# Second-phase weight sums formed during attention and kept in DRAM, x stored in 384-token pieces, eight output tiles in both passes

## The chip, the cores and the metric

The kernel runs on one core of a Trainium2 chip. The metric is the device time of one execution in microseconds. The engines are TensorE (PE in the profile, with its weight loads as PEld), VectorE (DVE), ScalarE (ACT), GpSimd (POOL, which here only issues accumulating DMAs) and SyncE (SP, which issues all other DMAs). Each engine, and each queue of DMA issues, works in the order in which its instructions were written.

## The reference

Linear attention with an exponential feature map (8 batches, 8 heads, 576 tokens, 64 dimensions, 128 features), and then a gated layer on the 4608 tokens of 512 features:

```python
def phi(x):
    proj = np.einsum('bhsd,df->bhsf', x, w_phi)
    proj = proj - np.max(np.abs(proj), axis=-1, keepdims=True)
    return np.concatenate([np.exp(proj), np.exp(-proj)], axis=-1)
q_p, k_p = (phi(q), phi(k))
kv = np.einsum('bhsf,bhsd->bhfd', k_p, v)
z = np.sum(k_p, axis=2)
num = np.einsum('bhsf,bhfd->bhsd', q_p, kv)
den = np.einsum('bhsf,bhf->bhs', q_p, z)[..., None] + 1e-06
...
gate = 1.0 / (1.0 + np.exp(-(x @ w_gate)))
val = x @ w_val
return (gate * val @ w_out).astype(np.float32)
```

The hidden width is 1536, twelve tiles of 128, called j = 0 to 11. The weights of the layer arrive as 64-bit floats.

## The kernel before

*Precision.* Every product of the gated layer is made of three matmuls: a value is split into a high part (a ScalarE copy that rounds) and a low part (a VectorE subtraction), and high x high, high x low and low x high are summed. `weigh` turns a raw 64-bit weight tile (512 KB, `raw`) into high and low with mask and shift operations on VectorE and two ScalarE operations.

*First phase.* There are 32 attention steps, one for a batch and a pair of heads (`attend`). The result x of a step goes to DRAM (`xscr`, the tile xs). As soon as 512 tokens are complete, `load_x` fetches them, splits them, sends high and low back to DRAM (`keep_x`, tile xparts), and `first_js` computes j = 0 to 3 for them, while attention goes on. Attention's last matmul stands at 516 us. Chunks 7 and 8 of the nine follow until about 617 us; I call this stretch the passage.

*Second phase.* The remaining eight j are taken in pairs n = 0 to 3, by a scheme with seven products in place of eight. For a pair and one of the three matrices m (gate, value, out), `combine` forms from two raw tiles, by sums and differences (lines L1103 to L1130), the high and low parts of seven weight blocks of 256 columns, one "sum" of 896 KB for each part. x enters in blocks of 768 tokens (two halves of 384): the four quarter blocks 11, 12, 21 and 22 give the seven operands 11, T1, T2, 21, T3, 22, T4 of the products (`x_blocks`). 11, 21 and 22 are fetched in high and low; the T operands are formed by VectorE (`less`, L1195; low part L1208) and ScalarE (L1204) from plain x. The 14 places for operands, `r_X`, hold one block and no more. The product matmuls all stand at L1250 (`group`); the copies that seed a product's bank are L1265 and the adds to a bank L1271.

Pass 1 runs n = 0, 1 over the six blocks (617 to 901 us), pass 2 runs n = 2, 3 (901 to 1200 us), starting with the block that pass 1 ended with, so that its x need not be fetched. A block is two gate groups, two value groups (the value group of the second pair is the last to read x) and four output groups (`sent`). An output group writes two tiles of 384 KB, which GpSimd adds to the output in DRAM with accumulating DMAs (L1404). In pass 1 the tiles (`r_w`) share places in the arena `flat` with gates and temporary values; in pass 2 eight tiles lie in an area of their own, `third`. Six sums are formed in the passage, for pass 1. One each is formed in the blocks 1 to 5 of pass 1 and stored to DRAM in both parts (`kept`, L1143), to be fetched for pass 2 (`fetched`, L1154); the twelfth is formed at the start of pass 2.

*Order.* Nothing is ordered by hand. `Plan.run` simulates the engines with costs per instruction and writes each engine's instructions in the order in which the simulation starts them; ranks decide between those that are ready. Buffers are places in arenas, which the simulation hands out as they come free.

The order of fetches before, in `x_blocks` (b11, b21 and b22, plain x, lie in the low halves of the operands of the same name):

```python
        b11, b21, b22 = (at_[n][1] for n in ("11", "21", "22"))
        fetch(b11, xscr, xmark, 0, 0)
        fetch(b12, xscr, xmark, 0, 1)
        fetch(b22, xscr, xmark, 1, 1)
        fetch(b21, xscr, xmark, 1, 0)
```

Of the kernel before, what the change touches and what calls it, by code (L numbers as in the profile page):

```python
# [39 lines left out]
RB = 61 << 10  # L40
FB = 10 << 10
SB = 14 << 10
# [18 lines left out]
KEEP = 10.0  # L61
SPAN = 46.0
PASS = 43.8
ACTN = 0.2

# [78 lines left out]
class Op:  # L144
    def __init__(self, eng, busy, lag, fn, rank, mode, slack, bufs, after):
        self.eng, self.busy, self.lag, self.fn = eng, busy, lag, fn
        self.rank, self.mode, self.slack, self.bufs = rank, mode, slack, bufs
        self.wait, self.then, self.ready, self.opens = len(after), [], 0.0, ()
        for a in after:
            a.then.append(self)  # L150


class Plan:
# [30 lines left out]
    def run(self):  # L184
        free = dict.fromkeys(self.NEAR, 0.0)
        ready = {e: [] for e in free}
        mode, wire, late = None, 0.0, 0
# [30 lines left out]
        while left:  # L218
            best = None
            for e, cs in ready.items():  # L220
# [3 lines left out]
                first = min(t for t, _ in ts) + (ACTN if late and e == 'ACT' else self.NEAR[e])  # L224
# [6 lines left out]
                t, o = min((x for x in ts if x[0] <= first), key=key)  # L231
# [10 lines left out]
            free[o.eng] = t + o.busy  # L242
            if o.eng in ("SP", "POOL"):
                wire = max(wire, t) + o.lag / self.RATE[late] * 1e-6
                end = wire + self.LAND[late]
            else:
                end = t + o.busy + o.lag
# [27 lines left out]
def attention_moe(  # L275
# [54 lines left out]
    for hd in range(2):  # L330
# [4 lines left out]
    xscr = dram.tile([P, NC4, NT], F32, tag="xs", name="xs")  # L335
    xparts = dram.tile([2, P, NC4, NT], F32, tag="xp", name="xparts")
    gscr = {
        (n, m): dram.tile([2, P, 7 * 2 * P], F32, tag=f"g{n}{m}", name=f"g{n}{m}")
        for n in range(2, 4)
        for m in range(3)  # L340
        if (n, m) != (3, 2)
# [7 lines left out]
    staged = arena("prep", "staged", SB, F32R)  # L349
# [10 lines left out]
    r_top = x.ring(2, DM, U32)  # L360
    x = low()
# [6 lines left out]
    r_stage = staged().ring(2, 7 * 2 * P)  # L368
    r_x7 = high(42).ring(2 * NC4, CW)
    r_O2 = r_O[:]  # L370
    r_O += r_stage
# [4 lines left out]
    r_f2 = r_f  # L376
    r_w = flat().ring(5, 2 * HT) + flat(15).ring(2, 2 * HT)
    r_w2 = third().ring(8, 2 * HT)
# [23 lines left out]
    def on_act(n, fn, reads, writes, rank, after=()):  # L402
        return plan.op("ACT", 0.08 + n / 1200, 0.17, fn, reads, writes, rank, after=after)
# [16 lines left out]

    def keep_x(c, p, bufs, r):

        for n, x in enumerate(bufs):
            sp(
                256 << 10,
                lambda n=n, x=x: nc.sync.dma_start(
                    xparts[n, :, p, c * CW : c * CW + CW], x().bitcast(F32)
                ),
                [x], [(pmark[c], (p, n))], r,
            )  # L430

    closing, opening, feeding, exps = [], [], [], []

    def attend(i):
        b, p = steps[i]
        r, slack = due(i), 0.1 if i < 2 * NP else 0.5
        early, on_pe = i < NP, i < NQ
        rk, rn = (r + 11, r + 18) if i < NP else (r + KOFF, r + NOFF)
        banks = [r_a, r_g] if early else [r_a]
# [354 lines left out]
        while t < S:  # L794
            c, o = divmod(b * S + t, CW)
            wd = min(CW - o, S - t)
            sp(
                wd * 512,
                lambda t=t, wd=wd: nc.sync.dma_start(
                    xscr[:, p, b * S + t : b * S + t + wd], xp()[:, t : t + wd]  # L800
                ),
                [xp], [(xmark[c], (p, b))], rn + 7,
            )
            t += wd

    def weigh(j, m, r, deep, wh, wl, ms, part, after=(), again=False):
# [23 lines left out]
        if deep:  # L830
# [24 lines left out]
        on_act(  # L855
            DM, lambda: act.copy(wh()[:, ms], top().bitcast(F32)), [top], [(wh, part)], r,
        )
# [9 lines left out]
        else:  # L867
# [23 lines left out]
            src, a, b_ = raw, 1, 0  # L891
        dve(
# [17 lines left out]
    def load_x(c, r, rings, after=()):  # L910
        for p in range(NP):
            xh, xl = Buf([x[0] for x in rings], [P, CW]), Buf([x[1] for x in rings], [P, CW])
            xs[c, p] = xh, xl
            sp(
                256 << 10,
                lambda p=p, xl=xl: nc.sync.dma_start(
                    xl().bitcast(F32), xscr[:, p, c * CW : c * CW + CW]
                ),
                [xmark[c % NCH]], [xl], r, after,
            )  # L920
# [114 lines left out]

    for i in range(N):
# [35 lines left out]
    last.opens = [a().cells for a in (high, more, staged)]  # L1072
# [9 lines left out]
    KH = 2 * P  # L1082
    combined = []

    def pair(n):
        return JA + 2 * n, JA + 2 * n + 1

    def combine(n, m, r, rings, after):

        gh, gl = Buf(rings, [P, 7 * KH]), Buf(rings, [P, 7 * KH])  # L1090
        w = Buf([r_sum], [P, 4 * KH])

        def of(b, i, n=1):
            return b()[:, i * KH : (i + n) * KH]

        for i, j in enumerate(pair(n)):
            weigh(
                j, m, r + 3 * i, False, gh, gl,
                slice(2 * i * KH, 2 * (i + 1) * KH), i, after + combined[-1:], True,
            )  # L1100
            o_ = dve(
                DM,
                lambda i=i: vec.tensor_tensor(  # L1103
                    of(w, 2 * i, 2), of(gh, 2 * i, 2).bitcast(F32),
                    of(gl, 2 * i, 2).bitcast(F32), op=ALU.add,
                ),
                [(gh, i), (gl, i)], [(w, i)], r + 5,
            )
            opened = opened if i else o_
        p12, p21 = (1, 2) if m < 2 else (2, 1)  # L1110
        for o, a, b, op in (
            (3, p21, 3, ALU.add),
            (p21, 0, p21, ALU.subtract),
            (0, 3, 0, ALU.subtract),
            (p12, p12, 0, ALU.subtract),
        ):
            dve(
                KH,
                lambda o=o, a=a, b=b, op=op: vec.tensor_tensor(
                    of(w, o), of(w, a), of(w, b), op=op  # L1120
                ),
                [], [w], r + 5.5,
            )
        for o, i, part in ((4, 3, 2), (p21, p21, p21 // 2), (5, 0, 3), (6, p12, 4)):
            on_act(
                KH, lambda o=o, i=i: act.copy(of(gh, o), of(w, i)), [w], [(gh, part)], r + 6
            )
            dve(
                KH,
                lambda o=o, i=i: vec.tensor_tensor(  # L1130
                    of(gl, o), of(w, i), of(gh, o).bitcast(F32), op=ALU.subtract
                ),
                [w, (gh, part)], [(gl, part)], r + 6,
            )
        combined.append(opened)
        return gh, gl

    def kept(bufs, where, mark, r):

        for n, x in enumerate(bufs):  # L1140
            sp(
                x.shape[1] << 9,
                lambda n=n, x=x: nc.sync.dma_start(where[n], x().bitcast(F32)),  # L1143
                [x], [(mark, n)], r,
            )

    def fetched(rings, width, where, mark, r, after=()):

        out = []
        for n in range(2):  # L1150
            x = Buf(rings, [P, width])
            sp(
                width << 9,
                lambda n=n, x=x: nc.sync.dma_start(x().bitcast(F32), where[n]),  # L1154
                [(mark, n)], [x], r, after,
            )
            out.append(x)
# [383 lines left out]
```

## Time and profile before

| | us |
|---|---|
| median of 3 runs (lowest, highest) | 1202.79 (1199.7, 1206.44) |
| the profiled execution, and its span | 1201.93, 1200.2 |
| first phase, to attention's last matmul | 0 to 516 |
| passage | 516 to 617 |
| pass 1 | 617 to 901 |
| pass 2 | 901 to 1200 |

Busy time is the union of an engine's instructions. A wait is idle time of an engine just before an instruction, put down to what released it last. A matmul shows some 0.34 us, but matmuls overlap, so the pace is read from counts and starts. The chain of waits follows the execution back from its last instruction.

### The profile page before, as it was taken

Reading aid. Unit: us, or ns where it says so; the run is one execution under the profiler, and the core shown is the slowest. Engines: PE = TensorE matmul, PEld = TensorE weight load, DVE = VectorE, ACT = ScalarE, POOL = GpSimd, SP = SyncE. Lnnn points to the kernel's source line nnn. Section 1 sums busy time; section 2 is a strip of 40 time slices with the busy share of each in tenths; the row PEclk is TensorE's granted clock in tenths of the full one; section 3 lists DMA queues with packets and bytes.
Section 4 is the critical chain, followed back from the end, with each engine's and each line's share of the span. In section 5 each row is a group of like instructions: output and inputs, shape, how many; then the busy total and the mean of one; then the engine's idle time right before and its main releaser. Section 6 shows DMA issues by size and latency. Waiting matters only on the chain.

```text
span 1200.2 us, 23363 instructions
## 1 busy us (share of the span) xinstructions
PE 1148.7 (96%) x8940; PEld 959.9 (80%) x8940; DVE 926.5 (77%) x1841; ACT 728.7 (61%) x1485; POOL 77.8 (6%) x94
## 2 busy tenths in 40 slices
PE   8989999999999999999999999799999898988988
PEld 6656667667776777778888989799899798988988
DVE  7998898888888787578899889497867575745746
ACT  6766776666666675435557667476655565645643
POOL 0000000000000000000001021110211202202010
PEclk9989999999999999999999999899999999998989
DMA  6863483645455362455647876868796827757371
GB/s 233 252 230 96 148 260 100 224 125 187 125 174 170 112 222 64 172 193 201 181 126 191 246 176 201 224 154 257 177 380 160 188 93 145 173 135 166 95 182 53
DMA packets 109784, 209.69 MB, mean 175 GB/s; under 512 B 19432, under 2 KB 54888, under 8 KB 109672
## 3 DMA queue, kind: packets, MB, share of 16 engines
q1 hardware_dynamic: 97000, 173.59, 43.5%
q0 software_dynamic: 12672, 34.61, 16.2%
q8 instruction: 70, 1.15, 0.4%
q14 instruction: 42, 0.34, 0.1%
HBM read 124.78 MB, written 83.24 MB: 173 GB/s over the span
## 4 chain that ended last, share of the span: by engine, by line
PE 63%; DVE 18%; DMA 14%; issue 3%; ACT 2%; POOL 0%; SPq 0%; DVEq 0%; POOLq 0%; ACTq 0%
PE gate L944 13%; PE bank L1250 13%; DMA low<-xparts 8%; PE gate L1250 7%; PE gate L1001 6%; PE bank L647 5%; PE bank L689 4%; PE bank L458 3%; DMA out<-flat 3%; DVE low L1352 3%; PE bank L707 2%; PE bank L944 2%; DVE flat L1195 2%; DVE flat L1271 2%; PE bank L563 2%
## 5 line engine op out<-in xcount | busy, mean ns | idle before, releaser
L1250 PE MATMUL bank<-low,high 128*128 128x384 f32 x1302 | 253.6, 345 | 25.2 <-DMA low<-xparts 21.0
L1250 PEld LDWEIGHTS bank<-low,high 128*128 128x128 f32 x1302 | 232.4, 193 | 33.4 <-DMA low<-xparts 24.0
L944 PE MATMUL gate<-low 128*128 128x512 f32 x708 | 173.8, 399 | 5.5 <-ACT low L784 4.5
L944 PEld LDWEIGHTS gate<-low 128*128 128x128 f32 x708 | 131.9, 191 | 38.0 <-issue 5.3
L1250 PE MATMUL gate<-low,high 128*128 128x384 f32 x714 | 143.6, 343 | 7.3 <-DMA low<-xparts 5.8
L1250 PEld LDWEIGHTS gate<-low,high 128*128 128x128 f32 x714 | 127.7, 192 | 11.0 <-DMA low<-xparts 7.7
L505 ACT ACTIVATE ek<-ek 128x512 f32<-128x512 f32 (+1 forms) x192 | 95.3, 527 | 19.9 <-DVE ek L493 18.9
L1404 POOL DMA_DIRECT2D out<-flat x48 | 42.1, 985 | 868.3 <-DMA low<-xparts 648.1
L1250 PE MATMUL bank<-low 128*128 128x384 f32 x397 | 88.8, 338 | 1.9 <-DVE flat L1271 1.7
L1001 PE MATMUL gate<-low 128*128 128x512 f32 x372 | 89.3, 394 | 0.0
L1001 PEld LDWEIGHTS gate<-low 128*128 128x128 f32 x372 | 68.6, 188 | 14.5 <-issue 1.0
L1349 ACT CAST low<-flat 128x384 fp32r<-128x384 f32 x127 | 61.0, 514 | 21.6 <-DVE flat L1358 19.2
L1250 PEld LDWEIGHTS bank<-low 128*128 128x128 f32 x397 | 70.2, 188 | 4.2 <-DVE flat L1271 2.9
L647 PE MATMUL bank<-ek,vin 128*32 128x256 f32 x1240 | 73.2, 381 | 0.2 <-DVE mb L729 0.2
L1271 DVE TENSOR_TENSOR flat<-bank,flat 128x384 f32<-128x384 f32 x95 | 51.5, 552 | 24.6 <-PE bank L1250 19.5
L647 PEld LDWEIGHTS bank<-ek,vin 128*32 128x32 f32 x1240 | 37.5, 110 | 38.7 <-issue 7.8
L1358 DVE TENSOR_TENSOR flat<-flat,bank 128x384 f32<-128x384 f32 x26 | 14.3, 552 | 64.5 <-PE bank L1250 64.1
L464 DVE TENSOR_REDUCE mk<-bank 128x4 f32<-128x512 f32 (+1 forms) x92 | 48.8, 555 | 19.5 <-PE bank L458 19.2
L1352 DVE TENSOR_TENSOR low<-flat,low 128x384 fp32r<-128x384 f32 x112 | 59.1, 551 | 2.9 <-ACT low L1349 2.7
L968 ACT CAST low<-flat 128x512 fp32r<-128x512 f32 x36 | 22.3, 619 | 53.5 <-DVE flat L993 45.4
L1265 ACT COPY bank<-bank 128x384 f32<-128x384 f32 x80 | 37.3, 466 | 24.8 <-PE bank L1250 22.4
L1343 DVE TENSOR_TENSOR flat<-flat 128x384 f32<-128x384 f32 x96 | 51.0, 552 | 0.3
(220 smaller groups left out, 2219.8 us busy)
## 6 DMA issues: line engine op xcount, KB each, us to landing
low<-xparts SPq DMA_DIRECT2D x66, 384.0 KB
out<-flat POOLq DMA_DIRECT2D x48, 384.0 KB, 9.0
xparts<-low SPq DMA_DIRECT2D x64, 256.0 KB
out<-third POOLq DMA_DIRECT2D x40, 384.0 KB, 9.4
low<-xs SPq DMA_DIRECT2D x33, 384.0 KB
more<-w_moe SPq DMA_DIRECT2D x24, 512.0 KB
kin<-k SPq DMA_DIRECT2D x32, 320.0 KB
qin<-q SPq DMA_DIRECT2D x32, 320.0 KB
```

What stands on the lines that cost most here:

```text
L464: vec.tensor_reduce(mx, pk, axis=AX.X, op=ALU.max, apply_absolute_value=True)
L505: lambda g=g, sg=sg: act.activation(ek[g]()[:, :, sg * F : sg * F + F], ek[g]()[:, :, F:], AF.Exp, scale=1.0 - 2.0 * sg,),
L647: nc.tensor.matmul(o_[o : o + Q, : 2 * F], vx()[:, 2 * t + hd, o % D : o % D + Q], (e0, e1)[hd][:, t, :] if t < 4 else e2[:, 0, :], start= ...
L689: nc.tensor.matmul(nm()[o : o + Q, :], w()[:, sg, o : o + Q], es[sg]()[:, o // D, cs], start=sg == 0, stop=sg == 1, tile_position=(0, o),)
L944: nc.tensor.matmul(o(), a()[:, ws], x(), start=cc + n == 0, stop=cc == NC4 - 1 and n == 2,)
L1001: nc.tensor.matmul(acc(), w()[:, ms], a(), start=first and i == 0, stop=last and i == 2)
L1250: nc.tensor.matmul(o()[:, :HT], s()[:, ws], y, start=first and n + cc + i_ == 0, stop=n == len(terms) - 1 and cc == steps - 1 and i_ == 2, ...
L1271: HT, lambda: vec.tensor_tensor(at_(), p()[:, :HT], q(), op=ALU.add),
L1343: HT, lambda: vec.tensor_tensor(o(), a(), b(), op=ALU.subtract),
L1349: on_act(HT, lambda: act.copy(hh(), y()), [y], [hh], -100.0, after)
L1352: lambda: vec.tensor_tensor(hl(), y(), hh().bitcast(F32), op=ALU.subtract),
L1404: lambda f=f, y=y: nc.gpsimd.dma_start(final(f, dc), flat_y(y), accum_op=ALU.add),
```

## The change

1. *Sums are kept whole in DRAM.* `weigh` gets a variant (`whole`) that adds the low part back to the top part in 32 bits. `kept` forms a sum in one tile without splitting it and stores it once (896 KB). `fetched` loads it once and splits it with one ScalarE copy and one VectorE subtraction of 1792 elements. `combine` is gone.
2. *Eight of the twelve sums are formed during attention*, issued after steps 8, 11, 14, 17, 20, 23, 26 and 28 with the lowest priority (`BETWEEN`, `spare`); the other four follow in the passage. All twelve are fetched, six for each pass. In attention they use the places of `r_w1` in `flat` and the raw tiles of the first phase.
3. *x in DRAM* has the layout [128, 12, 2, 768]: a block half of 384 tokens of two feature tiles is one run of 3 KB in a partition. Stores and loads of 512-token chunks and of attention's results are cut at 384-token borders (`pieces`). The high and low parts are two DRAM tiles, xh and xl.
4. *Order of the x fetches*: 12, operand 11, then plain 11, 22, operand 21, plain 21, operand 22. Plain 11, 22 and 21 lie in the low halves of T1, T2 and T3.
5. *Output tiles*: two places `spare` and six in `third` are used from the second block of pass 1 on; the first block uses `spare` and the old shared ones.
6. *The planner* has new costs: 0.4 us for a SyncE issue in the second phase, a share of 0.33 for SyncE's transfers beside GpSimd's, and a delay of 12 us for the ScalarE copy of a fetched sum.

```diff
+BETWEEN = (8, 11, 14, 17, 20, 23, 26, 28)
+FIRST = tuple((n, m) for a in (0, 2) for n, m in ((a, 0), (a, 1), (a + 1, 0), (a + 1, 1), (a, 2), (a + 1, 2)))
...
-    xscr = dram.tile([P, NC4, NT], F32, tag="xs", name="xs")
-    xparts = dram.tile([2, P, NC4, NT], F32, tag="xp", name="xparts")
+    xscr, *xparts = (
+        dram.tile([P, 2 * NDC, 2, 2 * HT], F32, tag=n, name=n) for n in ("xs", "xh", "xl")
+    )
...
-    r_w = flat().ring(5, 2 * HT) + flat(15).ring(2, 2 * HT)
-    r_w2 = third().ring(8, 2 * HT)
+    r_y2 = spare().ring(2, 2 * HT)
+    r_w = r_y2 + flat().ring(5, 2 * HT) + flat(15).ring(2, 2 * HT)
+    r_w2 = r_y2 + third().ring(6, 2 * HT)
...
+    def pieces(t, n):
+
+        e = t + n
+        while t < e:
+            h, o = divmod(t, HT)
+            w = min(HT - o, e - t)
+            yield t, w, (lambda x, p, h=h, o=o, w=w: x[:, h, p // 2, p % 2 * HT + o :][:, :w])
+            t += w
...
+    def kept(n, m, r, after, early=False):
+
+        since = len(plan.ops)
+        w = Buf([r_w1 if early else r_w7], [P, 7 * KH])
...
+        for i, j in enumerate(pair(n)):
+            o_ = weigh(
+                j, m, r + 3 * i, False, None, None, slice(2 * i * KH, 2 * (i + 1) * KH), i,
+                after + combined[-1:], not early, w,
+            )
+            opened = opened if i else o_
+        p12, p21 = (1, 2) if m < 2 else (2, 1)
+        for o, a, b, op in (
+            (4, p21, 3, ALU.add),
+            (p21, 0, p21, ALU.subtract),
+            (5, 4, 0, ALU.subtract),
+            (6, p12, 5, ALU.subtract),
+        ):
...
+        sp(896 << 10, lambda: nc.sync.dma_start(gscr[n, m], w()), [w], [mark], r + 6)
+        for o in plan.ops[since:]:
+            o.spare = o.eng == "DVE"
...
+        if i in BETWEEN:
+            n = len(plan.ops)
+            kept(*FIRST[BETWEEN.index(i)], 1e4, [plan.ops[-1]], True)
+            early += plan.ops[n:]
...
-    fed = plan.op("X", 0.0, 0.0, lambda: None, after=feeding)
+    fed = plan.op("X", 0.0, 0.0, lambda: None, after=feeding + early)
...
+        sp(
+            896 << 10, lambda: nc.sync.dma_start(gl().bitcast(F32), gscr[n, m]),
+            [marks[n, m]], [gl], r, after,
+        )
+        on_act(7 * KH, lambda: act.copy(gh(), gl().bitcast(F32)), [gl], [gh], r, (), SLACK)
...
-                lambda: nc.sync.dma_start(x().bitcast(F32), src[:, 2 * K : 2 * K + 2, t : t + HT]),
+                lambda: nc.sync.dma_start(
+                    x().bitcast(F32).rearrange("p a b -> p (a b)"), src[:, 2 * dc + h, K]
+                ),
...
-        b11, b21, b22 = (at_[n][1] for n in ("11", "21", "22"))
+        b11, b22, b21 = (at_[n][1] for n in ("T1", "T2", "T3"))
         b12, t1, t2 = (Buf([r_tmp], [P, 2, HT]) for _ in range(3))
+        fetch(b12, xscr, xmark, 0, 1)
+        parts("11")
         fetch(b11, xscr, xmark, 0, 0)
-        fetch(b12, xscr, xmark, 0, 1)
+        less(t1, b12, b11)
+        split("T1", t1)
         fetch(b22, xscr, xmark, 1, 1)
...
+        split("T2", t2)
+        parts("21")
         fetch(b21, xscr, xmark, 1, 0)
...
```

Two places of the built order. The first is SyncE's queue in pass 2, the x fetches of one block (`low` is the arena of the operands, 128x768 the elements; in brackets the semaphores that a fetch waits for: DMAHW of earlier DMAs, PE, DVE). Before:

```order
L1184 DMA low<-xs 128x2x384 [waits DMAHW2_49,PE_49]
L1184 DMA low<-xparts 128x2x384 [waits DMAHW3_49]
L1184 DMA low<-xparts 128x2x384 [waits DMAHW4_49,PE_49]
L1184 DMA low<-xparts 128x2x384 [waits DMAHW5_49]
L1184 DMA low<-xparts 128x2x384 [waits DMAHW6_49,DMAHW0_49,DVE_49]
L1184 DMA low<-xparts 128x2x384 [waits DMAHW7_49,DMAHW1_49,DVE_49]
L1184 DMA low<-xparts 128x2x384 [waits DMAHW2_49,DVE_49]
L1184 DMA flat<-xs 128x2x384 [waits Activation_49]
```

Now, all of a block's fetches:

```order
L1215 DMA low<-xh 128x768 [waits DMAHW4_49,PE_49]
L1215 DMA low<-xl 128x768 [waits DMAHW5_49]
L1215 DMA low<-xs 128x768 [waits DMAHW6_49,PE_49]
L1215 DMA low<-xs 128x768 [waits DMAHW7_49,PE_49]
L1215 DMA low<-xh 128x768 [waits DMAHW0_49,DVE_49,PE_49]
L1215 DMA low<-xl 128x768 [waits DMAHW1_49]
L1215 DMA low<-xs 128x768 [waits DMAHW2_49,PE_49]
L1215 DMA low<-xh 128x768 [waits DMAHW3_49]
L1215 DMA low<-xl 128x768 [waits DMAHW4_49,DVE_49,PE_49]
L1215 DMA flat<-xs 128x768 [waits DMAHW5_49,DVE_49]
```

Before, the last three xparts fetches wait for VectorE's L1195 of the same block; now the two DVE waits are for L1241 of the block before, which wrote those places long ago, and the rest waits for the matmuls that free a place.

The second place is VectorE's queue in an attention step, from the nineteenth transposition (`mb<-pm`) of the maxima on. Before (L983, L988, L993 and L970 belong to the gates of j = 0 to 3):

```order
L606 STREAM_TRANSPOSE mb_667<-pm_550 128x1152
L988 SCALAR_TENSOR_TENSOR flat<-flat,gate_183 128x512
L613 TENSOR_TENSOR d_497<-d_497,mb_667 128x1152
L993 SCALAR_TENSOR_TENSOR flat<-flat 128x512
L626 TENSOR_TENSOR s_1977<-ek_225 128x512
L633 TENSOR_TENSOR su_2153<-s_1977 128x256
L970 TENSOR_TENSOR low<-flat,low 128x512
L626 TENSOR_TENSOR s_1977<-ek_227 128x512
L633 TENSOR_TENSOR su_2153<-s_1977 128x256
L464 TENSOR_REDUCE mk_193<-bank_144 128x1
```

Now, from the same transposition on (L1036, L1041 and L1046 are the gates', L637 is the old L606):

```order
L637 STREAM_TRANSPOSE mb_678<-pm_558 128x1152
L657 TENSOR_TENSOR s_2017<-ek_235 128x512
L644 TENSOR_TENSOR d_505<-d_505,mb_678 128x1152
L1036 TENSOR_SCALAR flat<-flat 128x512
L664 TENSOR_TENSOR su_2207<-s_2017 128x256
L809 TENSOR_TENSOR xp_623<-ex_688,rb_517 128x576
L786 TENSOR_SCALAR dn_449<-dn_449 128x9
L787 RECIPROCAL dn_449<-dn_449 128x9
L855 TENSOR_SCALAR flat<-flat 128x512
L1041 SCALAR_TENSOR_TENSOR flat<-flat,gate_191 128x512
L495 TENSOR_REDUCE mk_201<-bank_164 128x1
L1046 SCALAR_TENSOR_TENSOR flat<-flat 128x512
```

L855 and L882 are two of the seven operations on a raw tile of a sum; before, no such row stood between the first weights and attention's end. Of the twelve sums, five and a half are complete in VectorE's order at the last attention step's transposition. TensorE's order up to 617 us differs from the old one in two places, where 24 gate matmuls move behind one step's kv, num and den matmuls.

More of the change, by code (lines that the diff above doesn't have):

```diff
@@ L64 @@
 ACTN = 0.2
+SHARE = 0.33
 class Cells:
@@ L223, in run @@
                     continue
-                first = min(t for t, _ in ts) + (ACTN if late and e == 'ACT' else self.NEAR[e])
+                idle = IDLE if late else SLIP
+                first = min(t + idle * o.spare for t, o in ts)
+                first += ACTN if late and e == "ACT" else self.NEAR[e]
                 def key(x):
@@ L229, in key @@
                     return o.rank + STICK * off, t
-                t, o = min((x for x in ts if x[0] <= first), key=key)
+                t, o = min((x for x in ts if x[0] + idle * x[1].spare <= first), key=key)
                 if best is None or t < best[0]:
@@ L241, in run @@
                     b.slot.take()
-            free[o.eng] = t + o.busy
+            free[o.eng] = t + max(o.busy, ISSUE if late and o.eng == "SP" else 0.0)
             if o.eng in ("SP", "POOL"):
-                wire = max(wire, t) + o.lag / self.RATE[late] * 1e-6
-                end = wire + self.LAND[late]
+                size = o.lag / self.RATE[late] * 1e-6
+                if o.eng == "POOL":
+                    added = max(added, t + o.busy) + size
+                    end = added + self.LAND[late]
+                else:
+                    s_ = max(wire, t)
+                    both = min(max(0.0, added - s_), size / SHARE)
+                    wire = s_ + both + size - both * SHARE
+                    added += size * (both > 0)
+                    end = wire + self.LAND[late]
             else:
-                end = t + o.busy + o.lag
+                end = t + o.busy + o.lag + (LAG if late else 0.0)
             if o.eng == "PE":
@@ L1138, in kept, with fetched @@
[L1138 to L1157, printed above, removed]
-        return out
+    def fetched(rings, n, m, r, after=()):
+        gh, gl = Buf(rings, [P, 7 * KH]), Buf(rings, [P, 7 * KH])
+        sp(
+            896 << 10, lambda: nc.sync.dma_start(gl().bitcast(F32), gscr[n, m]),
+            [marks[n, m]], [gl], r, after,
+        )
+        on_act(7 * KH, lambda: act.copy(gh(), gl().bitcast(F32)), [gl], [gh], r, (), SLACK)
+        dve(
+            7 * KH,
+            lambda: vec.tensor_tensor(gl(), gl().bitcast(F32), gh().bitcast(F32), op=ALU.subtract),
+            [gh], [gl], r,
+        )
+        return gh, gl
@@ L1474, in attention_moe @@
                 sent(sources, dc, m, r + 29.2 + 7.3 * (m if final_ else i), banks, final_)
-        if first and makes[n]:
-            key = makes[n]
-            mark = marks[key] = Buf()
-            kept(combine(*key, r + KEEP, [r_O], [done]), gscr[key], mark, r + KEEP)
-        ends = [o for o in plan.ops[since:] if o.eng in ("PE", "SP")]
     order = plan.run()
```

229 lines of the change are left out of this document (106 added, 123 removed).

## The prediction

> **What bounds the kernel now.** I read the page first, then the busy times by stage, the waits of TensorE after 617 us, and one block boundary of the second phase in four views. The page:
>
> ```profile
> span 1200.2 us, 23363 instructions
> PE 1148.7 (96%) x8940; PEld 959.9 (80%) x8940; DVE 926.5 (77%) x1841; ACT 728.7 (61%) x1485; POOL 77.8 (6%) x94
> ```
>
> TensorE carries the span, so a time can only fall where TensorE stands still or runs at a lower clock. Busy time by stage (the columns are PE, PEld, DVE, ACT and POOL with their counts, then granted clock, DMA share, GB/s): attention from step 12 on, the passage, a block of pass 1, the block of pass 1 with the longest stall, the first block of pass 2, and the later ones:
>
> ```profile
> core 0: us, PE busy (x) PEld busy (x) DVE busy (x) ACT busy (x) POOL busy (x), PEclk, DMA share, GB/s
> 197.00:516.00 319.00, 319.00 (x3185) 224.75 (x3180) 255.02 (x528) 199.04 (x388) 0.00 (x0) 1.00 0.47 152
> 516.00:617.00 101.00, 100.16 (x455) 82.68 (x448) 87.54 (x161) 51.16 (x94) 0.00 (x0) 1.00 0.61 200
> ...
> 617.00:901.00 284.00, 268.04 (x1480) 256.86 (x1479) 231.02 (x452) 180.86 (x386) 38.48 (x44) 0.99 0.76 214
> ...
> 752.00:806.00 54.00, 46.34 (x252) 45.63 (x251) 38.48 (x75) 30.91 (x66) 6.96 (x8) 0.94 0.70 186
> ...
> 901.00:945.00 44.00, 44.00 (x252) 43.30 (x251) 35.94 (x70) 29.95 (x68) 7.14 (x8) 1.00 0.66 154
> 945.00:996.00 51.00, 45.95 (x254) 44.94 (x253) 29.59 (x55) 27.74 (x59) 7.02 (x8) 0.97 0.59 140
> 996.00:1044.00 48.00, 44.80 (x255) 43.80 (x254) 29.78 (x55) 28.01 (x59) 7.05 (x8) 1.00 0.63 150
> 1044.00:1094.00 50.00, 45.90 (x253) 44.87 (x252) 29.36 (x55) 27.58 (x58) 7.02 (x8) 0.97 0.60 141
> 1094.00:1145.00 51.00, 46.68 (x253) 45.70 (x251) 29.38 (x55) 27.81 (x58) 6.99 (x8) 0.93 0.59 140
> ...
> 1145.00:1185.00 40.00, 36.35 (x192) 35.71 (x192) 18.03 (x37) 16.70 (x36) 3.45 (x4) 0.91 0.48 118
> ```
>
> Up to 617 us TensorE never rests. Afterwards a block has 252 matmuls; the block that takes over its predecessor's x (901 to 945) needs 44 us, the others 47 to 54, with nearly the same busy time. What TensorE's weight loads waited for in that phase (us in total, times, longest):
>
> ```profile
> PEld bank L1250 <- DMA low<-xparts: 24.0, 9, 7.2
> PEld bank L1250 <- DVE flat L1271: 9.1, 17, 1.2
> PEld gate L1250 <- DMA low<-xparts: 7.7, 6, 3.7
> PEld bank L1250 <- ACT bank L1265: 4.6, 7, 0.9
> PEld gate L1250 <- ACT gate L1265: 3.0, 5, 0.9
> PEld gate L1250 <- DVE flat L1271: 2.0, 4, 1.0
> ```
>
> The largest item is the fetch of x: 24.0 + 7.7 = 31.7 us. How it arises, at the boundary near 945 us: SyncE's queue, two pieces of the chain of waits, TensorE's own timeline, and the DMA queues from 925 to 930 and from 943 to 953 us:
>
> ```profile
> 924.00 1.58 SPq L1184 DMA_DIRECT2D low<-xs  x3
> 925.63 17.72 SPq L1184 DMA_DIRECT2D low<-xparts  x6
> ...
> 941.69 0.95 DVE flat L1195
> 942.64 0.03 DVE low L1352
> 942.67 13.68 DMA low<-xparts
> ...
> 945.25 3.28 PE L1250 MATMUL bank<-low,high 128*128 128x384 f32 x18
> ...
> 956.39 1.97 PE L1250 MATMUL bank<-low,high 128*128 128x384 f32 x5 [3.33 <-DMA low<-xparts]
> 958.16 1.85 PE L1250 MATMUL gate<-low,high 128*128 128x384 f32 x6
> ...
> q1 hardware_dynamic: 976, 1.42, 93.6%
> ...
> q0 software_dynamic: 534, 1.48, 78.0%
> q1 hardware_dynamic: 622, 0.91, 27.5%
> ```
>
> The nine fetches start at 924, when the last use of the old x frees its places, but the last of them is issued only at 942.67, after VectorE's subtraction L1195 has read the plain x that lies where that half of x must go. By then the accumulating output DMAs hold 78% of the DMA engines: the fetch takes 13.68 us. Just after 925 the same queue moved 1.42 MB in 5 us alone.
>
> Each long wait is paid twice. Six matmuls take 1.85 us at 958, against 3.28 us for 18 at 945. The clock rows price this as (1 - clock) x length: 0.06 x 54 + 0.03 x 51 + 0.03 x 50 + 0.07 x 51 + 0.09 x 40 = 13.4 us. The stage 996 to 1044 had a shorter wait and kept clock 1.00:
>
> ```profile
> PEld bank L1250 <- DMA low<-xparts: 2.9, 1, 2.9
> ```
>
> The Trainium skill, "TensorE: Matmul & The Clock Gate", section "HAM oscillation — how this bites in real kernels", says that idle gaps beyond about 3.4 us send the clock to half. These rows agree (3.33 us dropped it, 2.9 us did not). By that rule the whole 13.4 us goes as soon as the waits are merely halved; by the rows alone I would take back only what belongs to waits that vanish.
>
> **The change, part by part.** All terms stand against the profiled execution, 1201.9 us (span 1200.2); the median of the runs is 0.9 us more, which I ignore.
>
> *x fetches of the second phase.* Plain x now goes to places that no later DMA fills (the low halves of T1, T2, T3), and the order is that of need. In the built order none of the ten loads waits for this block's VectorE work; the places come free between the "11" and "22" products of the last value group, the stretch in which nine loads were queued in 5.5 us before. Ten loads of 384 KB at 1.42 MB per 5 us are 13.8 us, from 924 to about 938, when the output DMAs of the block begin; the next block begins at 945, and at 3.28 us for 18 matmuls, six to a product, it comes to its sixth product, "22", 5.5 us later. So the 31.7 us should go; the bounds are 0 (if something else holds the loads back; a loss is excluded, since no load waits for more than before) and 31.7. I take 31.7, and 13.4 of clock with it. What is late next are the T blocks made by VectorE and ScalarE and the seed copies L1265 (4.6 + 3.0 us, unchanged). I give back 4 us for the T blocks, between 0 and one L1208-sized wait (0.95 us) at each of ten boundaries.
>
> *x in 384-token pieces.* A partition's piece is one run of 3 KB where it was two of 1.5 KB. From 943 to 953 the queues alternate almost packet for packet (534 and 622), so a packet of twice the size would bring x twice as far beside output. Since the loads now fall ahead of the output DMAs, I count nothing; the cover is the 7 us from 938 to 945. The price is in attention: 128-token remainders, and 132 more DMAs on SyncE (607 to 739), nearly all before 617 us.
>
> *Weight sums.* An old sum has three mask operations and four full ones for each of its two raw tiles, then eight of 256 elements; a new one has three and four for each, then four. Their durations (the first row is min/median/max in ns, the others busy us, mean ns, idle before):
>
> ```profile
> L823 DVE TENSOR_SCALAR more<-more x24: 416/420/462, 533.9 to 907.8; 128x512 uint32<-128x512 uint32 x24
> ...
> L850 DVE SCALAR_TENSOR_TENSOR more<-more 128x512 uint32<-128x512 uint32 x24 | 16.6, 690 | 7.7 <-ACT more L827 7.6
> ...
> L1119 DVE TENSOR_TENSOR more<-more 128x256 f32<-128x256 f32 x48 | 20.3, 423 | 1.2
> ...
> L1208 DVE TENSOR_TENSOR low<-flat,low 128x768 fp32r<-128x768 f32 x44 | 41.6, 951 | 0.0
> L1352 DVE TENSOR_TENSOR low<-flat,low 128x384 fp32r<-128x384 f32 x112 | 59.1, 551 | 2.9 <-ACT low L1349 2.7
> ```
>
> Old: 2 x (3 x 0.42 + 4 x 0.69) + 8 x 0.42 = 11.4 us; new: 9.7 us. A fetched sum needs one subtraction of 1792 elements: 0.55 to 0.95 us for 384 more elements, so about 2.0 us, and a ScalarE copy that I put at the same.
>
> *Attention.* By the built order 5.5 sums finish before the last attention step's transposition: 53 us into 319 - 255 = 64 us of VectorE idle time from 197 us on. TensorE's order there is the old one but for two small swaps. The idle time is waiting for TensorE and ScalarE, the kind that a fixed order can fill; each inserted operation can hold up a due one by at most its own 0.69 us. With the 5.5 sums come eleven loads of 512 KB and 5 or 6 stores of 896 KB, some 11 MB: 34 GB/s beside 152, a DMA share of about 0.57, which hides them. Bounds 0 (TensorE is full, so nothing can be gained) and 53 us; I take 3, near 0, since VectorE still fits.
>
> *Passage, 516 to 617.* Six old sums (69 us) leave, 6.5 new ones (63) and six splits (12) come: +6 us beside 13.5 us of idle time. SyncE has the last stores, twice as many x pieces and four sum fetches ahead of the first x. Bounds 0 and 12 us (the sums of 6 us made twice late, by VectorE and by the queue); I take 3.
>
> *Pass 1.* Five sums (57 of VectorE's 231 us), ten stores and ten raw loads go, the sixth sum leaves the block at 901, and output tiles no longer share places with gates. The waits on L1271 (11.1 us) are bounded by 0 and 11.1; I take back 4. At the pass boundary six splits of 2 us come, under VectorE's idle time there (8 us of 44 in the block at 901 even with a sum in it): 0 if hidden, 12 if not; I take 1.
>
> Sum: 1201.9 - 31.7 - 13.4 + 4 + 3 + 3 - 4 + 1 = 1163.8, say 1164 us.
>
> **Rivals.**
>
> *Attention turns VectorE-bound, or the passage starts late (0.18).* For it: 11 us of spare VectorE time in 319 is little, and the waits below, small as they are, count when nothing is spare. Against: 6.9 of the 10.3 us arise in one wait, so most steps had none (VectorE, 197 to 516 us):
>
> ```profile
> DVE dn L755 <- DMA dn<-dr: 10.3, 5, 6.9
> DVE xp L778 <- DMA rb<-den: 7.7, 8, 5.0
> ```
>
> It costs 10 to 25 us on top of the 6 counted: 1174 to 1189.
>
> *Slower (0.07).* The sums sit in VectorE's fixed order, and each begins with a wait for a raw-weight DMA that stands in SyncE's fixed order among stores that wait for VectorE. If each holds up the other, the 53 us come on top of the attention stage instead of into its gaps, and the passage's 12 with them: 1164 + 50 + 9 = 1223. From 45 us of such loss on, the gain is gone. Against: VectorE waited for DMAs 18 us in 319, and TensorE was busy in all of the 319. The Trainium skill, "DMA: Bandwidth & Descriptors", section "Measured (HBM→SBUF, 128 partitions, SWDGE, issued from GpSimd)", counts transfers under 64 KB as descriptor-dominated, and speaks against cutting x into pieces. By its figures (0.95 us for 64 KB) some 130 more pieces are an estimated 120 us of DMA time; the DMA share of 0.47 in attention leaves 169 us free, so even that would be hidden, and no run here shows it.
>
> *The x waits stay (0.08).* If the loads still land during the output DMAs, only the L1271 waits and some clock go: 1190 to 1203. Against: the nine queued loads at 924 show that places and bandwidth are there.
>
> **How the numbers follow.** The forecast, 1152 to 1175, has 0.67. The range reaches through the first rival: 1150 to 1188, leaving out the slower case, the stay of the x waits and the ends. A measurement tells this kernel from no change at about 0.5%, 6 us. Faster: 0.67 + 0.18 + 0.02 of the x case = 0.87; same 0.06; slower 0.07.
>
> **What would show it.** Right: no wait of TensorE on an x fetch above 1 us after 617, blocks of 44 to 46 us in both passes, clock 1.00 from 617 on; x loads queued in one go of 5 to 8 us, with none behind L1228; attention's end at 516 to 520 us; VectorE busy above 93% from 197 to 516. Wrong: attention ending after 525 (the first rival), SyncE waiting for sums while VectorE waits for raw weights (the slower one), or x loads still beside output DMAs.

## The result, and the profile after

The changed kernel takes 1164.82 us (median of 4 runs, 1164.06 to 1165.6), against 1201.24 for the kernel before (4 runs): a ratio of 0.9692, interval 0.9656 to 0.9728. The profiled execution took 1164.7 us, its span is 1163.0. The forecast was 1164. The sum came out for a partly wrong reason, though: the terms for attention and passage were 8 us too low together, and those for the second phase gave 8 us too little gain, as the stages show.

The page, and the stages (columns as in the prediction's second view): attention from step 12 on, the passage, a block of each pass.

```profile
span 1163.0 us, 23394 instructions
PE 1134.9 (98%) x8940; PEld 952.9 (82%) x8940; DVE 925.3 (80%) x1805; ACT 712.7 (61%) x1425; POOL 77.9 (7%) x94
```

```profile
197.00:523.00 326.00, 321.89 (x3215) 225.69 (x3211) 308.15 (x654) 206.97 (x404) 0.00 (x0) 1.00 0.61 192
523.00:617.00 94.00, 88.02 (x370) 69.78 (x367) 74.42 (x122) 37.82 (x57) 0.00 (x0) 0.96 0.71 247
...
673.00:717.00 44.00, 44.00 (x254) 43.75 (x254) 28.07 (x54) 27.06 (x59) 6.38 (x8) 1.00 0.62 147
...
982.00:1026.00 44.00, 44.00 (x254) 43.77 (x253) 29.46 (x55) 27.12 (x59) 7.03 (x8) 1.00 0.67 161
```

Every block now takes 44 to 45 us, as only one block did before, at clock 1.00. Attention and the passage, full before, now have TensorE idle: 4 us of 326, and 6 of 94, with the clock at 0.96 in the passage. What TensorE's weight loads wait for after 617 us:

```profile
PEld bank L1283 <- DVE spare L1304: 1.3, 1, 1.3
PEld gate L1283 <- ACT gate L1298: 1.1, 2, 1.0
PEld bank L1283 <- DVE third L1304: 0.8, 2, 0.5
PEld gate L1283 <- DVE low L1385: 0.7, 3, 0.3
PEld bank L1283 <- DVE flat L1304: 0.6, 3, 0.2
```

No row names a fetch of x: 31.7 us are gone. The waits on L1304 (L1271 before) fell from 11.1 to 2.7 us, those on L1298 (L1265) from 7.6 to 1.3. SyncE's queue for the block that starts at 938 us (start, length, line, tiles) shows why:

```profile
917.33 0.32 SPq L1215 DMA_DIRECT2D low<-xh  x1
...
921.96 0.32 SPq L1215 DMA_DIRECT2D low<-xl  x1
934.29 0.32 SPq L1215 DMA_DIRECT2D flat<-xs  x1
```

And the DMA queue from 917 to 929 us (packets, MB, share):

```profile
q1 hardware_dynamic: 1283, 3.51, 83.0%
```

The nine loads are queued within 5 us, 16 us ahead of the block, and have the DMA engines to themselves (3.51 MB in 12 us). The fetch into `flat` at 934.29 is already for the block after.

Here are the kernels of this study by stage. The stage ends are starts of matmuls in TensorE's timeline of each profiled execution; the last column is the eleven blocks after the first.

| kernel | median us | attention ends | first block ends | other eleven |
|---|---|---|---|---|
| before | 1201.24 | 516.2 | 659.0 | 537.3 |
| changed | 1164.82 | 522.8 | 673.2 | 485.6 |
| order_only | 1160.49 | 518.8 | 658.9 | 499.0 |
| old_order | 1188.25 | 521.6 | 672.2 | 505.1 |
| layout_only | 1183.34 | 520.0 | 669.8 | 509.9 |
| no_between | 1225.12 | 518.1 | 714.5 | 499.4 |
| old_layout | 1150.44 | 516.8 | 656.9 | 485.5 |
| out_first | 1160.66 | 520.1 | 670.0 | 485.3 |
| issue_all | 1156.45 | 514.3 | 663.4 | 485.0 |
| old_tiles | 1172.30 | 522.8 | 673.6 | 490.5 |
| places_only | 1158.87 | 517.0 | 659.5 | 493.8 |
| sequence_only | 1173.79 | 519.0 | 661.8 | 509.4 |
| best | 1150.91 | 518.1 | 658.8 | 485.0 |
| best_out | 1149.96 | 518.3 | 659.0 | 486.1 |

The kernel before ran again beside each of three sets of experiments, with medians of 1197.81 (order_only to no_between), 1199.08 (old_layout to old_tiles) and 1199.39 us (the last four rows); the ratios below are to these. The changed kernel did not run again, so that a difference of a few us between its median and that of an experiment is less sure than it looks.

Before, order_only, places_only and sequence_only have the same first phase, and their attention ends at 516.2, 518.8, 517.0 and 519.0. So up to 3 us there tell nothing.

### The profile page after: what moved, and what is told of

It is laid out like the page before. It is cut to its first block, busy times and chain, and to the rows that moved or that the text cites. A ratio compares the mean times of both kernels' runs of the same rounds, so it can differ in the third digit from the quotient of the medians.

```text
span 1163.0 us, 23394 instructions
## 1 busy us (share of the span) xinstructions
PE 1134.9 (98%) x8940; PEld 952.9 (82%) x8940; DVE 925.3 (80%) x1805; ACT 712.7 (61%) x1425; POOL 77.9 (7%) x94
## 4 chain that ended last, share of the span: by engine, by line
PE 71%; DVE 16%; DMA 7%; ACT 2%; issue 2%; SPq 2%; DVEq 0%; ACTq 0%
PE bank L1283 29%; PE gate L1283 15%; PE gate L997 8%; PE gate L1054 4%; PE bank L678 3%; DMA rb<-den 3%; PE bank L720 2%; PE bank L489 2%; DMA low<-xs 1%; PE bank L1054 1%; DVE mb L637 1%; PE bank L738 1%; PE bank L594 1%; DVE pm L616 1%; PE bank L997 1%
## 5 line engine op out<-in xcount | busy, mean ns | idle before, releaser
L1283 PE MATMUL bank<-low,high 128*128 128x384 f32 x1338 | 246.8, 336 | 0.0
L1283 PE MATMUL gate<-low,high 128*128 128x384 f32 x678 | 130.9, 336 | 0.6 <-ACT gate L1298 0.6
L1283 PEld LDWEIGHTS gate<-low,high 128*128 128x128 f32 x678 | 118.6, 188 | 1.1 <-ACT gate L1298 1.1
L1283 PE MATMUL bank<-low 128*128 128x384 f32 x523 | 116.8, 339 | 1.2 <-DVE spare L1304 1.0
L1283 PEld LDWEIGHTS bank<-low 128*128 128x128 f32 x523 | 92.7, 188 | 4.4 <-DVE spare L1304 1.3
L1437 POOL DMA_DIRECT2D out<-third x60 | 52.7, 1177 | 350.8 <-DVE third L1304 266.2
L1304 DVE TENSOR_TENSOR flat<-bank,flat 128x384 f32<-128x384 f32 x74 | 40.4, 554 | 40.9 <-PE bank L1283 34.1
L1391 DVE TENSOR_TENSOR flat<-flat,bank 128x384 f32<-128x384 f32 x39 | 21.4, 550 | 61.2 <-PE bank L1283 61.2
L1437 POOL DMA_DIRECT2D out<-spare x22 | 19.4, 881 | 686.5 <-DVE flat L1376 662.9
L1283 PE MATMUL gate<-low 128*128 128x384 f32 x267 | 65.1, 338 | 0.0
L1298 ACT COPY bank<-bank 128x384 f32<-128x384 f32 x81 | 37.8, 467 | 33.7 <-PE bank L1283 32.2
```

The costliest lines, as they stand in the source:

```text
L1283: nc.tensor.matmul(o()[:, :HT], s()[:, ws], y, start=first and n + cc + i_ == 0, stop=n == len(terms) - 1 and cc == steps - 1 and i_ == 2, ...
L1298: HT, lambda: act.copy(o()[:, :HT], src()[:, :HT]), [src], [o], -200.0, before
L1304: HT, lambda: vec.tensor_tensor(at_(), p()[:, :HT], q(), op=ALU.add),
L1437: lambda f=f, y=y: nc.gpsimd.dma_start(final(f, dc), flat_y(y), accum_op=ALU.add),
```

## The experiments

**The new order and places of the x fetches, alone (order_only).** In the kernel before:

```diff
-        b11, b21, b22 = (at_[n][1] for n in ("11", "21", "22"))
+        b11, b22, b21 = (at_[n][1] for n in ("T1", "T2", "T3"))
...
+        fetch(b12, xscr, xmark, 0, 1)
+        parts("11")
         fetch(b11, xscr, xmark, 0, 0)
-        fetch(b12, xscr, xmark, 0, 1)
...
```

> The kernel before with the new order and places of the x fetches alone (old layout, old sums, old output tiles). Theory A (the prediction's: the last three loads waited for VectorE's subtraction and so fell among the output DMAs): TensorE's waits on x after 617 us fall from 31.7 to under 3 us, blocks of both passes take 44 to 46 us, attention and passage end where they did before (516 and 617 us), 1150 to 1165 us in all. Rival B (the 3 KB pieces brought the gain): about half the waits stay, 10 to 20 us, 1175 to 1195 us. Rival C (VectorE freed of the sums in pass 1 brought a good part): pass 2 has blocks of 44 to 45 us, the first pass keeps 46 to 50, 1165 to 1175 us.

Measured: 1160.49 us, ratio 0.9678 (0.961 to 0.9747). These few lines give the whole gain of the change. The waits after 600 us:

```profile
PEld bank L1250 <- ACT bank L1265: 7.9, 11, 1.6
PEld bank L1250 <- DVE flat L1271: 4.8, 10, 1.0
PEld gate L1250 <- ACT gate L1265: 3.6, 3, 1.5
```

No wait on x is left, with rows of 1.5 KB, which refutes rival B. Rival C holds in part: blocks of pass 2 take 44 us, those of pass 1, with a sum in each, still 46 to 48.

**The old order in the changed kernel (old_order)**, the same lines turned back.

> The changed kernel with the old order and places of the x fetches alone. Theory A: the waits on x come back, 15 to 32 us with the lost clock on top, blocks of 46 to 52 us, 1185 to 1210 us. Rival B (3 KB pieces double the share of x beside output): waits under 8 us, clock 1.00, 1165 to 1177 us. Rival C: as B in pass 1, waits in pass 2 only.

Measured: 1188.25 us, 23 us slower than the changed kernel. The waits on x come back, but below theory A's range:

```profile
PEld gate L1283 <- DMA low<-xl: 6.7, 4, 2.1
PEld bank L1283 <- DMA low<-xl: 6.5, 5, 1.8
```

SyncE's queue near 932 us hangs on three fetches for 14 us, as it did before:

```profile
931.81 13.98 SPq L1215 DMA_DIRECT2D low<-xl  x3
```

And over the stage from 617 to 1177 us the clock is 1.00 in the mean (it falls in one block, shown further on):

```profile
617.00:1177.00 560.00, 542.12 (x3058) 532.02 (x3058) 368.76 (x662) 335.71 (x687) 77.19 (x88) 1.00 0.62 156
```

The cause is back. That less comes of it than before points at the layout, which the next run shows alone.

**x in 384-token pieces, alone (layout_only).** The kernel before with the three new DRAM tiles and `pieces`.

> The kernel before with x stored in 384-token pieces alone (old order of fetches, old sums). Theory A: within 8 us of before, 1195 to 1208 us: waits on x a little shorter, and the first phase 0 to 5 us longer by the additional DMAs on SyncE. Rival B: 1165 to 1185 us. The end of attention and of the passage shows what the pieces cost there: 0 to 2 us in attention if the changed kernel's 6.6 us there come from the sums, 5 to 7 if they come from the pieces.

Measured: 1183.34 us, ratio 0.9844 (0.9756 to 0.9932). Neither theory foresaw it: the second phase gains 27 us, with the fetches still held back (13.54 us of queue at 937), and the first block ends 11 us later. The chain of waits at the boundary near 953 us, to be held against the 13.68 us that the same fetch took before:

```profile
949.21 0.96 DVE flat L1209
950.17 0.02 issue
950.19 9.94 DMA low<-xl
```

L1209 (the old L1195) ends 2.6 us ahead of the block, as it did before. The fetch after it is 3.7 us shorter, so TensorE waits for x for 8.9 us in all in place of 31.7. Why it is shorter is not settled: beside the output DMAs x's queue brought 0.94 MB in 10 us (950 to 960) in 339 packets, before 0.91 MB in 622, and over the whole of the fetch 0.96 MB in 9.94 us against 1.12 MB in 13.68. So the bytes per time rose by 3 to 18%, and not to the double: the prediction's reading that the queues alternate packet for packet does not hold for the larger ones (339 beside 523 of output). Its sum did not use it.

**New places alone, and new sequence alone (places_only, sequence_only)**, both in the kernel before. In the first the operand T3 is formed from plain 22 after T2's low part has overwritten it; in the second the low halves of 11 and 21 hold plain x. So neither gives the layer's result, and only their times are read; the work and the number of transfers are the same.

```diff
# places_only
-        b11, b21, b22 = (at_[n][1] for n in ("11", "21", "22"))
+        b11, b22, b21 = (at_[n][1] for n in ("T1", "T2", "T3"))
```

> The kernel before with the new places of plain x alone (low halves of T1, T2, T3, which no later fetch fills); the sequence of the fetches stays. It parts the two halves of the new order. Theory A (the wait of three fetches for L1195 is what counted): waits on x fall under 6 us, 1160 to 1170 us. Rival D (the sequence, need first, is what counted, and the wait for VectorE was a bystander): 15 to 30 us of waits on x stay, 1180 to 1200 us.

> The kernel before with the new sequence of the x fetches alone; plain x stays in the places of its own operands, so that fetches still wait for L1195. Theory A: at least the last fetches fall among the output DMAs as before, waits on x of 10 to 30 us, 1180 to 1200 us. Rival D: waits under 6 us, 1160 to 1170 us.

Measured: 1158.87 (ratio 0.9654, 0.9626 to 0.9683) and 1173.79 us (0.9779, 0.975 to 0.9808). The place of plain x is what counts: with it alone no wait on x is left, and the queue passes in one go. The sequence was no bystander either: alone it brought a good part, which neither forecast had. But as built it was not a clean trial: it also reduced the fetches that wait for VectorE from three to one (the last, at 945.16), and it kept 4.1 us of waits on x. SyncE's queue in places_only, then in sequence_only:

```profile
914.69 3.54 SPq L1184 DMA_DIRECT2D low<-xparts  x6
...
921.77 0.36 SPq L1184 DMA_DIRECT2D flat<-xs  x1
```

```profile
929.90 0.41 SPq L1184 DMA_DIRECT2D low<-xparts  x1
930.56 4.45 SPq L1184 DMA_DIRECT2D low<-xs  x2
945.16 0.36 SPq L1184 DMA_DIRECT2D low<-xparts  x1
```

**The old layout in the changed kernel (old_layout)**: `pieces` goes, the rest of the change stays.

```diff
-        for t, w, of in pieces(c * CW, CW):
...
-                lambda: nc.sync.dma_start(
-                    x().bitcast(F32).rearrange("p a b -> p (a b)"), src[:, 2 * dc + h, K]
-                ),
+                lambda: nc.sync.dma_start(x().bitcast(F32), src[:, 2 * K : 2 * K + 2, t : t + HT]),
```

> The changed kernel with x in DRAM laid out as before (runs of 1.5 KB, no cuts at 384 tokens); sums, order of fetches, output tiles stay. Theory A (the new order alone removed the waits on x; the cut-up stores on SyncE cost most of the 14 us that the first block now ends later): the first block ends at 660 to 665 us in place of 673, TensorE's waits on x stay under 2 us, blocks of 44 us in both passes, 1148 to 1157 us. Rival B (the first phase grew because of the sums on VectorE): the first block ends at 670 to 674, 1161 to 1167 us. Rival C (beside the sums' fetches the small packets matter): 5 to 15 us of waits on x come back, 1158 to 1172 us.

Measured: 1150.44 us (1148.34 to 1152.81), ratio 0.9616 (0.9566 to 0.9665): 14.4 us less than the changed kernel, with blocks of 44 us and no waits on x. By the ratios (0.9616 against 0.9692) it is some 9 us, with intervals that just touch; best, further on, has the same layout and lies clear of the changed kernel. Theory A holds, and the first block ends even earlier than it said, at 656.9 us. Attention and passage are full again, although VectorE does the same sums there:

```profile
197.00:517.00 320.00, 320.00 (x3203) 225.57 (x3201) 306.13 (x650) 207.20 (x403) 0.00 (x0) 1.00 0.58 194
517.00:600.00 83.00, 83.00 (x367) 68.11 (x364) 72.41 (x118) 36.97 (x56) 0.00 (x0) 1.00 0.77 278
```

VectorE is busy in 306 of 320 us, and TensorE shows no idle time: a stage filled to 96% by its second engine did not become bound by it.

**No sums in attention (no_between)**: `BETWEEN = ()`.

> The changed kernel with no sum in attention: all twelve follow in the passage. If the 6.6 us that attention grew come from the sums' operations on VectorE, attention ends at 516 to 518 us; if from the cut-up x stores, at 521 to 523. The eight sums (78 us of VectorE) then stand in the passage, where about 20 us are idle: it grows by 45 to 60 us, 1200 to 1220 us in all. If sums that pass 2 needs can be left until pass 1, where VectorE is idle a third of the time, only the first six press, and it is 1180 to 1190.

Measured: 1225.12 us, above both ranges. Attention ends at 518.1, within the scatter; the first block ends 41 us later than in the changed kernel, for 78 us of additional VectorE work. The longest waits of TensorE from 518 to 714 us:

```profile
PEld bank L1283 <- ACT low L1184: 26.1, 2, 14.4
PEld bank L1283 <- DVE low L1187: 8.5, 2, 4.3
PEld bank L1283 <- ACT high L1184: 6.3, 1, 6.3
```

TensorE waits for the splits of fetched sums, which are not yet there. VectorE's idle time in attention is thus worth some 60 us to the sums (1225 - 1165) in this kernel.

**The output stores first (out_first)**: the rank of L1083 set to -100.

> The changed kernel, with the output stores of the first phase (L1083) ranked ahead of all else on SyncE. Theory A (in the passage the stores stand behind some 50 x stores of 0.43 us each; ScalarE waits 8.5 us at L1077 for a place that they free, and TensorE 6 us after that): the wait at L1077 falls under 3 us, the first block ends 4 to 6 us earlier, at 667 to 669, 1158 to 1161 us. Rival: the passage is bound by VectorE's own work (sums and splits), the first block ends at 671 to 674 as before, 1162 to 1166 us.

Measured: 1160.66 us. The time is as theory A has it (the ratio, 0.97, is that of the changed kernel), but its mechanism is not: the waits at L1077 still sum to 7.9 us, and from the end of attention to that of the first block it takes 149.9 us, 150.4 in the changed kernel. The 2.7 us came in attention, within the scatter, though two of TensorE's three waits there (1.3 and 0.9 us in the changed kernel) have fallen to 0.2 us and nothing. The stores' place in the queue is not what holds the passage.

**SyncE's issues reckoned at 0.4 us throughout (issue_all)**: the planner's `if late` goes.

```diff
-            free[o.eng] = t + max(o.busy, ISSUE if late and o.eng == "SP" else 0.0)
+            free[o.eng] = t + max(o.busy, ISSUE if o.eng == "SP" else 0.0)
```

> The changed kernel, whose planner reckons 0.4 us for every SyncE issue from the start, in place of 0.06 us before the second phase. Theory A (SyncE's queue is what the plan misjudges in passage and attention): the order puts urgent transfers ahead, the first block ends 2 to 6 us earlier, 1158 to 1163 us. Rival: the order hardly changes and with it the time, 1163 to 1167 us.

Measured: 1156.45 us, better than expected; its four runs (1154.26 to 1159.13) all lie below the changed kernel's, but the ratio, 0.9673 (0.9613 to 0.9732), does not tell the two apart. The passage is no shorter (149.1 us); attention ends 8.5 us earlier, of which 3.4 stand by the 900th matmul, ahead of any sum. So the reckoning, if it helps, does so in another place than the one named.

**Output tiles of pass 1 shared with gates, as before (old_tiles).**

> The changed kernel with the output tiles of pass 1 in places shared with gates, as before; eight tiles in pass 2 only. Theory A (a good part of the 11.1 us of waits on L1271 came from tiles that a store still held): the waits on L1304 rise from 2.7 to 6 to 11 us, blocks 2 to 5 take 45 to 46.5 us in place of 44.0, 1168 to 1175 us. Rival B (those waits went because VectorE has no sums in pass 1 any more): blocks of 44.0 to 44.5, 1164 to 1167 us.

Measured: 1172.30 us, 7.5 more than the changed kernel. Theory A holds in the sum (7.1 us of waits on L1304); the place is another, chiefly one wait of 4.1 us in the last block of pass 1, and blocks 2 to 5 stay near 44 us:

```profile
PEld bank L1283 <- DVE flat L1304: 6.2, 4, 4.1
```

**Both gains together (best, best_out).** old_layout with issue_all's line, and with out_first's as well.

> The changed kernel with x laid out as before and with 0.4 us per SyncE issue reckoned from the start: the two edits that gained 14 and 8 us apart. If both took the same loss (SyncE's queue full of cut-up x stores), together they give what the layout alone gave, 1147 to 1152 us. If the reckoning also orders the start better (the changed kernel with it was 3.6 us ahead at the 900th matmul), 1140 to 1147 us.

> The kernel called best with the output stores of the first phase (L1083 of the changed kernel) ranked first as well. Without the cut-up stores there is little in front of them: ScalarE waited 2.7 us for such places in the passage. 0 to 3 us less than best; a rise would say that the x fetches behind them matter more.

Measured: 1150.91 (ratio 0.9585, 0.9562 to 0.9608) and 1149.96 us (0.9575, 0.9551 to 0.96). Neither differs from old_layout by what can be told: the planner's reckoning helped, if at all, only where there were pieces to put in order. The version that beats both kernels is the changed one with the old layout of x, about 1150 us.

## Why the prediction was right, and where it was not

*The x fetches (-31.7 and -13.4 us): right, and shown.* The waits went in full with the place of plain x alone, came back in part with the old order (13.2 us beside the new layout), and the loads stand as forecast: nine in 5 us, none behind VectorE's subtraction, clock 1.00.

*The clock.* By the rows alone I would have taken back only what belongs to vanished waits. old_order tells the two readings apart: it keeps 13.2 of the 31.7 us of waits, by which 13.4 x 13.2 / 31.7 = 5.6 us of half clock should stay, yet after 617 us the clock falls in one block alone, by 0.04 x 48 = 1.9 us:

```profile
855.00:903.00 48.00, 45.87 (x254) 45.24 (x253) 28.17 (x51) 28.74 (x58) 6.97 (x8) 0.96 0.64 185
```

So most of the lost clock went with the shortening of the waits. In layout_only two blocks fell, the deeper one to 0.93:

```profile
763.00:814.00 51.00, 46.77 (x252) 46.05 (x252) 38.63 (x75) 30.87 (x65) 7.18 (x9) 0.93 0.71 196
```

and in it lies one wait of 4.3 us:

```profile
PEld bank L1264 <- DMA low<-xl: 4.3, 1, 4.3
```

The length of one wait does not decide it, though, as the prediction had it with its 3.33 and 2.9 us (the first is idle time of the matmuls, the second of the weight loads; the matmuls' own was 2.58 us there). Falls of the clock followed idle times of the matmuls of 3.04 us (before, at 1152 us), 2.17 us (sequence_only, at 910 us) and 1.52 us (old_order, at 860 us), and none followed 2.58 us (before, at 1003 us) or 2.48 us (sequence_only, at 1130 us). What the traces share is this: within a run the falls begin whole multiples of 3.41 us apart. Of the 21 falls between 200 us and the end of the matmuls, in all fourteen traces, 20 follow a stretch of that grid in which TensorE was busy for at most 1.54 of the 3.41 us, and one a stretch with 1.9 us; the least busy stretch without a fall has 1.7 us. By this it is the idle time within one stretch that counts, which is inferred from these traces and was not tried by a run. The Trainium skill, "TensorE: Matmul & The Clock Gate", section "HAM oscillation — how this bites in real kernels", names idle gaps beyond about 3.4 us. It was the better guide for the sum; as a limit for one gap these traces do not bear it out.

*The T blocks (+4): not needed.* No wait on L1241 shows up. *L1271 (-4, L1265 0): too small.* They fell by 8.4 and 6.3 us. old_tiles gives 7.5 us of the total to the eight tiles; the rest probably came with the sums' leaving pass 1 (order_only, which keeps them, has 7.9 + 3.6 us of waits on L1265, and old_tiles, which does not, 2.3). *The pass boundary (+1): right*, the block from 893 takes 45.2 us in place of 44.3. The eleven blocks lost 51.7 us against 44.1 forecast; the waits that fell sum to more than that (46.4 us, and 13.4 of clock), as waits are booked on the weight loads, which run ahead of the matmuls.

*Attention and passage (+3 and +3): the step that failed.* They grew by 6.6 and 7.6 us; attention ended at 522.8 us, between the prediction's signs of right (516 to 520) and of wrong (after 525). That TensorE never rests up to 617 us was true from 130 us on only (10.7 us of idle time lie ahead of that), but nothing hung on it. I put the risk on VectorE's sums, and gave the cut-up x no price of its own. In the passage it is the other way round: with the sums and without the pieces (old_layout) the first block ends 2 us earlier than before, and with the pieces and without sums in attention or splits (layout_only) 11 us later. The passage shows one stall in the changed kernel and in layout_only, here TensorE in the two:

```profile
580.40 0.19 PEld L1054 LDWEIGHTS bank<-low 128*128 128x128 f32 x1 [1.54 <-ACT low L1021]
...
585.45 0.29 PEld L1054 LDWEIGHTS bank<-low 128*128 128x128 f32 x1 [3.93 <-ACT low L1021]
```

```profile
PEld bank L1014 <- ACT low L981: 4.8, 2, 3.4
```

All seven kernels with the pieces have it (matmuls idle for 3.0 to 3.5 us at one place between 571 and 586 us, and half clock for 3.4 or 6.8 us there), and none of the seven without. From the end of attention to that of the first block it takes 149 to 151 us with the pieces (no_between, with all its sums there, aside) and 140 to 143 us without. So the pieces bring it.

In the 50 us after attention SyncE issues 68 transfers (33 us of issues), in old_layout 45 (21 us). In attention 3.6 of the 6.6 us arise at three waits of TensorE after 204 us (the rest, before, is within the scatter). They stand only where both are there: no kernel with the pieces alone (layout_only, no_between) or with the sums alone (old_layout, best, best_out) has the matmuls idle for more than 0.5 us at a time there. Nor has issue_all, which has both in another order. In the chain of the second, 1.1 us at 315 us, stands an operation of a sum (L939, 0.58 us), as the prediction had feared. The last of them, followed back by the chain of waits (420 to 431 us):

```profile
422.04 0.05 issue
422.09 0.43 SPq L831
422.52 0.05 issue
422.57 0.42 SPq L831
...
423.09 0.39 SPq L969
423.48 0.04 issue
423.53 3.37 DMA low<-xs
...
426.97 0.62 ACT low L975
427.59 1.05 ACT ek L536 x2
428.64 0.37 ACT kvt L699
429.01 0.04 issue
429.06 0.55 PE bank L704 x3
```

The x stores of a step (L831) delay the x fetch (L969) in SyncE's fixed order; ScalarE's copy of it (L975) holds up the exponentials and the kvt copy behind it, and these hold up TensorE. The prediction had asked what stands behind a waiting instruction for the sums, and not for the pieces. The Trainium skill, "DMA: Bandwidth & Descriptors", section "Measured (HBM→SBUF, 128 partitions, SWDGE, issued from GpSimd)", which it cited, counts transfers under 64 KB as descriptor-dominated. The added pieces have 64 KB and more, and old_layout shows that they cost 14.4 us all the same; as DMA time that section's figures don't give this, since the DMA share in attention was 0.61.

In which way the pieces bring the passage's stall, by the issues' own time or by the smaller packets, is open; out_first only excludes the place of the output stores. The sums' operations between L1018 and L1023 in VectorE's order can't be enough, since old_layout and best have sums in the passage and no stall.

*The rivals.* The first (a late first phase) came true by half and from another cause, and its 8 us were paid by what the other terms had too little. The slower case's mechanism, sums and stores holding up each other, hardly appeared: VectorE waited once in attention, 4.1 us, for a raw weight.

## What to carry to other kernels

When a fetch is late, look at what its place waits for before looking at bandwidth: three loads stood behind a subtraction only because another operand had been put into their place, and putting it elsewhere was worth as much as the whole change. Idle time of an engine could here be filled to 96% with work that is in no hurry, although that work also put 24 large transfers into SyncE's fixed queue (16 of 512 KB, 8 of 896 KB); what cost was to put 132 small ones into it. And a sum that comes out right proves none of its terms: compare by stage.

## What was not expected of the hardware

A DRAM layout of 3 KB rows in place of 1.5 KB cut the last held-back fetch, at the boundary shown, from 13.68 to 9.94 us beside accumulating output DMAs, and the waits on x from 31.7 to 8.9 us, while the bytes that x's queue moved per time rose by 3% (0.91 and 0.94 MB in the first 10 us) to 18% (over the whole fetch). The kernels whose TensorE waits longest for such fetches also scatter more: 1188.94 to 1208.07 us for the kernel before (35 runs) and 1182.22 to 1194.48 for old_order (10 runs), against spreads of 1.5 to 5.8 us, in four to six runs each, for the eleven kernels other than these two and layout_only (8.9 us).

The granted clock fell at places whole multiples of 3.41 us apart, after stretches of that grid with little work, and once after an idle time of only 1.52 us.
